# Two convolution blocks issued one step earlier, their writes put ahead of the reads, and one transposing 128x128 transfer beside the first loads

## Chip, cores, metric

One core of a Trainium2 chip. The metric is the device time of the program in microseconds (us), lower is better. Each timed run also leaves the span of the profiled part, which is about 1.8 us shorter than the time. A ratio below is the mean time of one kernel's fast runs over the mean of the other's fast runs of the same rounds, so not quite the ratio of the medians that are quoted beside it.

## The reference

```python
# attention part: a causal 7-tap convolution over the sequence, one softmaxed filter per head
x: (8, 4096, 192); weight: (8, 7)           # 8 heads of 24 channels
w = softmax(weight, axis=-1)
att[b, s, h] = sum_k w[h, k] * x_pad[b, s + k, h]     # zero padding of 6 in front
# MoE part, over the 32768 tokens
h = att @ w_in                              # 192 -> 2048
g = where(h > 0, h, exp(min(h, 0)) - 1)     # ELU
out = g @ w_out                             # 2048 -> 192
```

## The kernel before

The tokens are worked off in 32 super-tiles of 1024. Each has 16 steps; a step multiplies one block of 128 hidden columns into PSUM (`H<-att,w_in`), ScalarE takes the exponential, GpSimd clamps it, VectorE makes the ELU (`gT`), and the second product (`ops<-w_out,gT`) is interleaved. Between steps stand convolution blocks for later super-tiles, each for one half (`g`) of 512 tokens. Their results go to DRAM (`bounce`, in the profile `conv_slots`) and come back in another layout as `att`. Super-tile 0 has a path of its own at the start: x is loaded, cast, transposed and convolved on the spot.

```python
EARLY_CONV = {4: (1, 0), 7: (1, 1), 10: (2, 0)}   # after step n: convolve (super-tile, half)
...
def load_first(eng, k):                       # one half of the first x tile, DRAM to xf
    eng.dma_start(xf[:, k, :, :]..., x_flat[GS * k : GS * (k + 1), :]...).then_inc(s_xl[k], 16)

def read_att(eng, W, s, g):                   # three loads of 64 KB: att of half g
    m = 2 * s + g - 2
    W(s_dw[m % 4], 16 * (m // 4 + 1))         # the write of this half has landed
    for j in range(3):
        eng.dma_start(att[HP * g : HP * (g + 1), s % 2, j, :], src).then_inc(s_att[s % 2], 16)
...
def _sync(sy):
    sy.dma_start(wh[:], weight[:, :]).then_inc(s_wd, 16)
    load_first(sy, 1)                         # the other half is loaded by the ACT queue
    W(s_wp, 1)
    sy.dma_start(taps[:, :], zt[:, :]).then_inc(s_band, 16)
    W(s_band, 16)
    sy.dma_start(Tr[:, :, :], <tap matrix out of taps>).then_inc(s_band, 16)
    W(s_w[3], 16)
    sy.dma_start(w_in[HP:P, :, c0:c1], w_in[0:HP, :, c0:c1]).then_inc(s_wc, 16)
    for item in order:
        if item[0] == "c":                    # a convolution block m
            conv_read(W, m)                   # evacuated into csb
            sy.dma_start(bounce[...], csb[:, m % 4, :, :]).then_inc(s_dw[m % 4], 16)
            if m == 0 or g == 1:
                read_att(sy, W, s, g)         # waits for the write just issued to land
        ...
# TensorE, at the start
warm(9)                                       # matmuls on zeros
...                                           # broadcast of the taps into H
W(s_xha, 1); W(s_xh, 1)                       # both x halves cast
...                                           # transposes of x, then the first convolution
```

## Time and profile before

| | before |
|---|---|
| time, median of 2 runs | 750.02 us (749.67 to 750.38) |
| the profiled run | 752.16 us, span 750.4 us |
| TensorE busy | 737.4 us, 98% |
| longest wait on the path | 2.8 us, step 16 for `att` |

The prediction shows the chain and the waits. Added here, from the order of time of the same profile (start us, length us, engine, line, operation, tiles, count; in brackets the idle time before and what ended it), is the start-up of TensorE: the first convolution in two groups of matmuls, and step 0.

```profile
7.83 1.06 PE L648 MATMUL ops<-xT,Dg 64*128 64x256 bf16 x16 [0.34 <-ACT xT L438]
8.71 1.94 PE L648 MATMUL H<-xT,Dg 64*128 64x256 bf16 x32
11.21 0.82 PE L706 MATMUL H<-att,w_in 64*128 64x512 bf16 x6 [0.56 <-ACT att L447]
```

The first convolution runs from 7.83 to 10.65, 2.82 us, and step 0 starts at 11.21. Below, these two numbers are the measure of a start.

### The profile page before, as it was taken

What the parts mean: (1) busy time and instruction counts of PE and PEld (TensorE: products, weight loads), DVE (VectorE), ACT (ScalarE), POOL (GpSimd) and SP (SyncE); (2) the same over time, 40 slices, a digit from 0 to 9 for tenths busy, and PEclk for the clock granted to TensorE, in tenths of its full rate; (3) what the DMA queues carried; (4) which work ended last, traced back from release to release, by engine and by line L of the source; (5) the groups of instructions that cost most, each with busy time, mean ns of one, the idle gap of its engine ahead of it and who ended that gap; (6) DMA issues with size and microseconds to landing.
All of it is one profiled execution on the core that took longest, in us unless ns stands there. A gap on an engine that the chain in (4) does not pass through costs nothing.

```text
span 750.4 us, 32212 instructions
## 1 busy us (share of the span) xinstructions
PE 737.4 (98%) x13850; PEld 518.0 (69%) x13850; DVE 637.9 (85%) x1041; ACT 646.7 (86%) x1165; POOL 659.7 (88%) x1107
## 2 busy tenths in 40 slices
PE   7799999999999999999999999999999999999998
PEld 4377777777777777776776776777776777777666
DVE  5779888889888888898898898898898898888894
ACT  5788888888888888888989888888888888888884
POOL 8779889899899899899898898898898898998883
PEclk9999999999999999999999999999999999999999
DMA  9644434534435435435435435435345444345212
GB/s 171 126 86 99 99 92 103 107 84 104 90 97 107 106 75 115 86 90 113 102 81 117 84 92 110 93 93 115 77 101 107 88 102 103 87 103 105 60 44 65
DMA packets 107038, 72.79 MB, mean 97 GB/s; under 512 B 44552, under 2 KB 106640, under 8 KB 106896
## 3 DMA queue, kind: packets, MB, share of 16 engines
q1 hardware_dynamic: 66384, 54.47, 24.0%
q0 software_dynamic: 40224, 15.78, 19.6%
q8 instruction: 108, 1.77, 1.0%
q10 hardware_dynamic: 288, 0.49, 0.2%
q14 instruction: 34, 0.28, 0.1%
HBM read 44.78 MB, written 41.42 MB: 115 GB/s over the span
## 4 chain that ended last, share of the span: by engine, by line
PE 96%; DMA 2%; ACT 1%; DVE 0%; SPq 0%; issue 0%; POOL 0%
PE ops L741 45%; PE H L706 45%; PE H L679 5%; DMA conv_slots<-csb 1%; PE H L741 1%; DMA xf<-in_x_dram 1%; DMA att<-conv_slots 0%; SPq L334 0%; DVE gT L561 0%; ACT E L499 0%; PE H L648 0%; PE ops L648 0%; ACT csb L479 0%; POOL E L410 0%; ACT xT L438 0%
## 5 line engine op out<-in xcount | busy, mean ns | idle before, releaser
L561 DVE SCALAR_TENSOR_TENSOR gT<-E,H 128x512 f16<-128x512 f32 x1024 | 632.8, 681 | 96.7 <-POOL E L410 90.5
L410 POOL TENSOR_SCALAR E<-E 128x512 f32<-128x512 f32 x1024 | 602.7, 612 | 78.2 <-ACT E L499 72.6
L499 ACT ACTIVATE E<-H 128x512 f32<-128x512 f32 x1024 | 546.2, 606 | 87.8 <-PE H L706 79.2
L741 PEld LDWEIGHTS ops<-w_out,gT 64*128 64x128 f16 x8064 | 346.1, 94 | 107.0 <-ACT osb L470 10.9
L741 PE MATMUL ops<-w_out,gT 64*128 64x192 f16 x8064 | 417.9, 243 | 0.3
L706 PE MATMUL H<-att,w_in 64*128 64x512 bf16 x3072 | 408.7, 377 | 5.3 <-DMA att<-conv_slots 2.8
L706 PEld LDWEIGHTS H<-att,w_in 64*128 64x128 bf16 x3072 | 133.9, 94 | 102.9 <-issue 5.2
L479 ACT ACTIVATE csb<-H 128x1024 bf16<-128x1024 f32 x59 | 60.4, 1023 | 0.0
L470 ACT ACTIVATE osb<-ops 128x768 f32<-128x768 f32 x63 | 51.6, 819 | 6.2 <-PE ops L741 6.2
L362 POOL DMA_DIRECT2D xg<-in_x_dram x62 | 52.5, 847 | 0.4 <-issue 0.4
L679 PE MATMUL H<-Tr,xg 128*24 128x122 bf16 (+1 forms) x2360 | 38.6, 209 | 0.0
L679 PEld LDWEIGHTS H<-Tr,xg 128*24 128x24 bf16 x2360 | 29.6, 92 | 9.3 <-issue 9.3
L741 PE MATMUL H<-w_out,gT 64*128 64x192 f16 x128 | 5.9, 243 | 0.0
L572 DVE COPY osb<-H 128x192 f32<-128x192 f32 x1 | 0.4, 358 | 6.3 <-PE H L741 6.3
L741 PEld LDWEIGHTS H<-w_out,gT 64*128 64x128 f16 x128 | 5.3, 94 | 0.0
L592 PE MATMUL ops<-zw 128*128 128x512 bf16 x9 | 4.0, 631 | 1.2 <-DVE zw L511 1.2
L367 POOL DMA_DIRECT2D w_in<-in_moe_w_in_dram x7 | 4.6, 657 | 0.3 <-DMA wh<-in_weight_dram 0.3
L597 PE MATMUL ops<-zw 64*128 64x512 bf16 x12 | 2.3, 379 | 1.6 <-ACT csb L479 1.6
L479 ACT ACTIVATE csb<-ops 128x512 bf16<-128x512 f32 x6 | 3.8, 625 | 0.0
L592 PEld LDWEIGHTS ops<-zw 128*128 128x128 bf16 x9 | 1.2, 142 | 3.2 <-issue 1.9
L597 PEld LDWEIGHTS ops<-zw 64*128 64x128 bf16 x12 | 0.6, 93 | 3.0 <-ACT csb L479 2.6
L679 PEld LDWEIGHTS ops<-Tr,xg 128*24 128x24 bf16 x120 | 1.5, 92 | 1.3 <-issue 1.3
(47 smaller groups left out, 25.9 us busy)
## 6 DMA issues: line engine op xcount, KB each, us to landing
out_dram<-osb SPq DMA_DIRECT2D x126, 192.0 KB, 2.7
conv_slots<-csb SPq DMA_DIRECT2D x62, 256.0 KB, 2.5
att<-conv_slots SPq DMA_DIRECT2D x186, 64.0 KB
xg<-in_x_dram POOLq DMA_DIRECT2D x31, 240.0 KB, 5.1
xg<-in_x_dram POOLq DMA_DIRECT2D x31, 192.0 KB, 4.5
w_out<-in_moe_w_out_dram POOLq DMA_DIRECT2D x1, 768.0 KB, 14.3
w_in<-in_moe_w_in_dram POOLq DMA_DIRECT2D x2, 240.0 KB, 7.9
xf<-in_x_dram ACTq DMA_DIRECT2D x1, 384.0 KB, 3.2
```

The source lines that it names most:

```text
L362: g.dma_start(xg[:, b, w0:w1, :], src).then_inc(s_x[b][part - 1], 16)
L367: g.dma_start(w_in[HP * r : HP * (r + 1), :, c0:c1], moe_w_in.rearrange("(p j) f -> p j f", j=3)[:, :, c0:c1],).then_inc(s_w[k], 16)
L410: g.tensor_scalar(out=E[:, n % NE, u, :], in0=E[:, n % NE, u, :], scalar1=1.0, scalar2=0.0, op0=ALU.min, op1=ALU.max,).then_inc(s_clp)
L470: a.activation(osb[:, b, :, :, :].rearrange("p g k d -> p g (k d)"), ops[:, :, 0 : 2 * D], ACT.Copy,).then_inc(s_oev)
L479: return a.activation(csb[:, m % 4, b0:b1, :], conv_bank(m)[:, b0:b1, :], ACT.Copy)
L499: a.activation(E[:, n % NE, u, :], H[:, k, GS * u : GS * (u + 1)], ACT.Exp).then_inc(s_exp)
L561: v.scalar_tensor_tensor(out=gT[:, s % NG3, q, u, :], in0=E[:, n % NE, u, :], scalar=1.0, in1=H[:, slot_of_pair[n] % 3, GS * u : GS * (u + ...
L592: pe.matmul(ops[:, 0, :], zw[:, 0:P], zw[:], start=True, stop=True)
L597: pe.matmul(ops[:, r, :], zw[HP * r : HP * (r + 1), 0:P], zw[HP * r : HP * (r + 1), :], start=True, stop=True, tile_position=(HP * r, 0),)
L679: ins = pe.matmul(to[SLOT * q : SLOT * q + CPH, hb, o : o + nc_], xg[:, s % NXB, w, CPH * h : CPH * (h + 1)], Tr[:, h, CW - c0 - nc_ : CW ...
L706: ins = pe.matmul(H[:, k % 3, GS * r : GS * (r + 1)], w_in[HP * r : HP * (r + 1), j, FC * q : FC * (q + 1)], att[HP * r : HP * (r + 1), s ...
L741: ins = pe.matmul(acc[:, g, d0 : d0 + D], gT[HP * rt : HP * (rt + 1), t % NG3, q, g, t0 : t0 + P], w_out[HP * rt : HP * (rt + 1), q, :], s ...
```

## The change

Its intent: the write of half 1 shall no longer queue behind the reads of half 0, and both halves shall be ready earlier. A transposing transfer from SBUF to SBUF is added besides; nothing reads its result. Its source is a tile of zeros.

```diff
-EARLY_CONV = {4: (1, 0), 7: (1, 1), 10: (2, 0)}
+EARLY_CONV = {3: (1, 0), 6: (1, 1), 10: (2, 0)}
...
+        tt = sbuf("tt", [P, P], BF16)
...
+        s_tx = sema("s_tx")
...
             sy.dma_start(wh[:], weight[:, :]).then_inc(s_wd, 16)
+            W(s_zw, 1)
+            sy.dma_start_transpose(out=tt[:, 0:P], in_=zw[:, 0:P]).then_inc(s_tx, 16)
             load_first(sy, 1)
...
-                    if m == 0 or g == 1:
-
+                    if m == 1:
+                        read_att(sy, W, s, 0)
+                    if g == 1:
                         read_att(sy, W, s, g)
...
+            W(s_tx, 16)
```

## The prediction

> **What bounds the kernel now.** I read the page's engine table first, then the chain of work that ended last (whole, then its first 70 us), then the longest waits and the table by stretches of the same time, then the order of time around the stall, and last the DMA queues microsecond by microsecond.
>
> The engine table of the page:
>
> ```profile
> PE 737.4 (98%) x13850; PEld 518.0 (69%) x13850; DVE 637.9 (85%) x1041; ACT 646.7 (86%) x1165; POOL 659.7 (88%) x1107
> ```
>
> TensorE is busy for 737.4 of 750.4 us. From 43 us on the stretches show it busy without a gap, so nothing there can be shortened by moving transfers: the steady state is a block of fixed length, and the change can only move the moment at which it begins. All that matters lies before 43 us. The chain there (start, length, what):
>
> ```profile
> 1.26 4.12 DMA xf<-in_x_dram
> 5.37 0.02 issue
> 5.40 0.57 DVE xh L536
> ...
> 19.87 5.74 DMA conv_slots<-csb
> 25.61 0.02 issue
> 25.62 0.67 SPq L334
> ...
> 27.58 2.55 DMA conv_slots<-csb
> ...
> 31.40 3.55 DMA att<-conv_slots
> 34.95 0.05 issue
> 35.00 0.82 PE H L706 x6
> 35.82 0.78 PE ops L741 x12
> 36.60 1.28 PE H L706 x6
> 37.88 1.57 PE ops L741 x20
> 39.45 0.65 PE H L706 x6
> ```
>
> It begins with the second half of the first x load, on the sync queue, and later runs through that queue: write of conv half 0 (landed 25.61), three reads of half 0 (issued 25.62 to 27.54), only then the write of half 1, its three reads, and at 34.95 the data that step 16, the first of the second super-tile, needs. The longest waits and the stretches (length; busy us and count of PE, PEld, DVE, ACT, POOL; granted clock; DMA share; GB/s) show what it costs:
>
> ```profile
> PE H L706 <- DMA att<-conv_slots: 2.8, 1, 2.8
> ```
>
> ```profile
> 32.00:35.00 3.00, 0.15 (x5) 0.01 (x2) 2.35 (x4) 0.78 (x2) 1.52 (x3) 1.00 0.45 138
> 36.00:37.00 1.00, 1.00 (x12) 0.68 (x10) 0.00 (x0) 0.95 (x2) 0.46 (x1) 0.50 0.00 0
> ```
>
> TensorE stands from 32.15 to 35.00, 2.85 us. Afterwards its granted clock is 0.50, and the groups of the chain take twice as long: 0.78, 1.28 and 1.57 us, where the same groups later take 0.49, 0.65 and 0.82. That is another 1.67 us. The stall so costs 4.5 us in all.
>
> Was the order on the sync queue to blame? In the order of time:
>
> ```profile
> 23.38 0.65 ACT L479 ACTIVATE csb<-ops 128x512 bf16<-128x512 f32 x1
> 27.58 0.45 SPq L773 DMA_DIRECT2D conv_slots<-csb  x1
> ```
>
> Half 1 was evacuated at 24.03, but its write was issued at 27.58: 3.55 us behind a wait for the landing of half 0 and three reads. And why did half 0 need 5.74 us, where later writes take 2.5? The queues (packets, MB, share), first from 20 to 21 us, then from 22 to 23:
>
> ```profile
> q0 software_dynamic: 502, 0.19, 159.8%
> ```
>
> ```profile
> q1 hardware_dynamic: 155, 0.23, 73.6%
> ```
>
> Up to about 21 us the weight and x loads issued by GpSimd fill the engines, and the sync queue (q1) moves nothing, though its copy of w_in was issued at 17.82. The write of half 0 can't land much before 25 however early it is issued.
>
> **What the skill says.** (1) The Trainium skill, "VectorE: DVE Perf Modes", section "The three transpose paths", gives the crossbar DMA 1309 ns for 128x128 bf16. This trace has no transpose; its plain sync issues take 0.36 to 0.40 us. (2) "DMA: Bandwidth & Descriptors", section "Queues, rings and completion order": on each DMA engine descriptors are consumed in ring order. So a transfer put ahead of the x load on the same queue is served ahead of it. The trace agrees: the conv_taps write, issued at 3.61, landed at 5.75, after the x load before it at 5.38. (3) The same page, section "Rules for kernel authors", says a transpose next to ordinary DMAs needs nothing; so I expect no corruption and no pause of the other queues, which no run has shown yet. (4) "TensorE: Matmul & The Clock Gate", Part 1: the array falls to half its clock after an idle window of about 3.4 us. The trace agrees on the half clock, but 2.85 us of standing sufficed here, and the half clock lasted from about 35.9 to 39.2.
>
> **The change part by part.** *Convs one step earlier.* Half 0 moves from after step 4 to after step 3, half 1 from after step 7 to after step 6. The input is there: the GpSimd queue landed x for half 0 near 12.7 us (issue 5.11 plus 7.6) and for half 1 near 16.4 (7.61 plus 8.8). ScalarE is close to fully busy from 18 to 31 and does the same evacuations in another order, so half 0 is ready perhaps 0.65 us earlier, near 19.2, and half 1 near 23.4. The number of warming matmuls stays 12. By itself this buys almost nothing, because of the DMA backlog above. Value: about 0.
>
> *Writes ahead of reads.* Half 1 is now written as soon as evacuated: issue near 23.4 to 24, in the ring right behind half 0. At the 0.2 MB per us that q1 reaches there, 0.25 MB more land by about 27, not 30.13. Reads of half 0: from 25.6, three issues, 1.92 us, to 27.5. Reads of half 1: 1.9 to 2.2 us more, to about 29.5; the last lands 2.6 us after the end of its issue, as before (34.95 minus 32.33), so at about 32.1 instead of 34.95. TensorE's own arrival was 32.15. The stall of 2.85 us goes, and with it the half clock: minus 2.85 minus 1.67, or minus 4.5 us. The elementwise engines don't take its place: VectorE finishes step 15 at 34.35 in the trace before, when step 18 would first need that buffer at about 35.
>
> *The transpose.* It is issued on the sync queue between the first two loads. Its source is filled at 1.19 us and the queue is free at 1.20, so its wait is free. It holds the queue for between 0.45 us (a little over a plain issue) and 1.3 us (the skill's figure taken as issue time), and its 32 KB are ahead of the x load in the ring. That load is the head of the chain. Pushed back by 0.5 to 1.3 us, more of it meets the GpSimd loads, which begin at about 4 us; in that microsecond q1 fell from 0.28 to 0.11 MB. I estimate that the x load lands 1.2 us later (0.6 to 2.5). The chain from there to step 0 has no slack, since VectorE waited 1.8 us for it; so the whole start moves by that. The reads of half 1 stay near 32.1, being held by the DMA backlog, while TensorE arrives at step 16 near 33.3, so the delay also secures that no stall is left. The final wait for the transpose is over long before the end and costs nothing.
>
> Sum: 750.0 - 4.5 + 1.2 = 746.7; with 0.1 for a remnant of a stall, 746.8 us.
>
> **Rivals.** *The transpose is dear.* A queue entry of another kind may hold the sync queue or the engines for several us. Nothing in the trace before speaks for or against it. With 3 us the time is about 748.5, with 4.5 about 750; if it went as 2-byte pieces (16,384 elements, some 1,000 per engine), at the roughly 30 per us and engine that 244-byte packets reach at 8 to 9 us, it would be over 30 us and the kernel over 2% slower. The skill's 1309 ns speaks against that. *The wait moves instead of going.* If reads of half 1 queue behind its write or their issue slows, att lands at 33 to 34; since TensorE comes late by the transpose's delay, at most about 1 us of stall is left: 747 to 748. *A cold start.* TensorE stands from 5.27 to 6.10 now; with the x load late it stands 2 us or more, and a window there could halve the clock for some us: plus 1.5, about 748. *All hidden.* If the x load does not feel the transpose (q1 moved nothing before 3 us anyway, behind the other half on the ACT queue), the whole 4.5 us remain: 745.5.
>
> **Range and chances.** The gain of 4.5 is measured and bounded; the transpose is the uncertain term. Delays of 0 to about 4 us give 745.4 to 749.4, which I take as the 8-in-10 range. Two per cent is 15 us: a gain that big isn't there to be had, so faster has 0.01; slower needs the 2-byte case or a stalled queue, 0.05; within 2% is 0.94.
>
> **What would show it.** Right: the wait of L706's line for att is gone or under 1 us; the granted clock is 1.00 from 32 to 40; two conv_slots writes stand together ahead of six att issues on the sync queue; the first cast of xf on VectorE begins near 6.6 instead of 5.40, and step 0 near 12.4 instead of 11.21. Wrong: a transpose issue of several us; the xf cast later than 8 us; a remaining att wait over 2 us, with the clock at 0.50 after it; or gaps in the steady state, which would mean that the transpose does something lasting to the queues.

## More of the kernel before

The experiments were timed in rounds with runs of the kernel before: e1 to e4, then e5, e6, e7 and e9, and then e8 with e10 to e12, on another chip.

## The result, and the profile after

The changed kernel took 750.75 us (750.67 and 750.83) against 750.02 before; the ratio is 1.0011 with an interval of 0.9987 to 1.0035. That is the same time, within 2% as forecast, but outside the predicted range of 745.4 to 749.4.

The sync queue of the changed kernel, in order of time:

```profile
1.26 1.21 SPq L759 DMA_TRANSPOSE tt<-zw  x1
2.52 0.57 SPq L301 DMA_DIRECT2D xf<-in_x_dram  x1
...
21.84 4.54 SPq L777 DMA_DIRECT2D conv_slots<-csb  x2
26.91 3.83 SPq L336 DMA_DIRECT2D att<-conv_slots  x6
```

The order is as intended: two writes (the length of a merged row spans the pause between them), then six reads, the last issued by 30.74. The `att` wait is gone. In the same table of stretches that showed a clock of 0.50 before, the changed kernel has:

```profile
36.00:37.00 1.00, 1.00 (x20) 0.64 (x18) 0.91 (x3) 1.00 (x2) 1.00 (x3) 1.00 0.28 88
```

So the whole 4.5 us that the prediction read out of the profile before are gone. What came in their place is at the start. From the order of time of the changed kernel:

```profile
6.60 0.56 DVE L538 CAST xh<-xf 128x768 bf16<-128x768 f32 x1 [3.02 <-DMA xf<-in_x_dram]
...
9.03 1.83 PE L650 MATMUL ops<-xT,Dg 64*128 64x256 bf16 x16 [0.33 <-ACT xT L440]
10.62 2.88 PE L650 MATMUL H<-xT,Dg 64*128 64x256 bf16 x32
...
14.06 0.82 PE L708 MATMUL H<-att,w_in 64*128 64x512 bf16 x6 [0.56 <-ACT att L449]
```

The transpose holds the sync queue for 1.21 us and the x load is issued 1.26 us later. The cast of x starts at 6.60 instead of 5.40, 1.20 us late. The first convolution then takes 4.47 us instead of 2.82, and its first group 1.83 instead of 1.06. Step 0 starts at 14.06 instead of 11.21, 2.85 us late. The stretches of the changed kernel (the column before the last two is the granted clock) name the cause of the second part:

```profile
9.00:10.00 1.00, 0.97 (x11) 0.87 (x13) 0.20 (x1) 0.37 (x1) 1.00 (x2) 0.56 1.10 108
10.00:11.00 1.00, 1.00 (x13) 0.87 (x10) 0.00 (x0) 0.10 (x1) 1.00 (x2) 0.50 1.50 189
```

The sum of this pair of profiles closes: minus 2.85 (stall) minus 1.67 (half clock after it) plus 2.85 (late start) plus 0.1 (a slightly longer way from step 0 to step 16) is minus 1.57, and the spans differ by 1.5 us. But the timed runs do not show minus 1.5. The profiled run of before took 752.16 us, about 2 us more than its timed runs. Which of the two stands for the kernel had to be found out.

### The profile page after: what moved, and what is told of

Same layout as the page of the kernel before. It is cut to its first block, busy times and chain, and to the rows that moved or that the text cites. A ratio compares the mean times of both kernels' runs of the same rounds, so it can differ in the third digit from the quotient of the medians.

```text
span 748.9 us, 32213 instructions
## 1 busy us (share of the span) xinstructions
PE 737.1 (98%) x13850; PEld 518.0 (69%) x13850; DVE 637.8 (85%) x1041; ACT 646.9 (86%) x1165; POOL 659.3 (88%) x1107
## 4 chain that ended last, share of the span: by engine, by line
PE 96%; DMA 2%; ACT 1%; DVE 1%; issue 0%; POOL 0%; ACTq 0%
PE ops L743 45%; PE H L708 45%; PE H L681 5%; DMA Tr<-conv_taps 2%; PE H L743 1%; DVE gT L563 0%; DMA conv_taps<-zt 0%; ACT E L501 0%; ACT csb L481 0%; ACT L425 0%; PE ops L681 0%; POOL E L412 0%; PE ops L599 0%; ACTq L301 0%; DVE osb L574 0%
```

## Experiments

**The theory.** Step 16 starts at the later of two moments: when TensorE arrives (step 0 plus some 20.8 us), and when `att` of super-tile 1 lands. In the old order the landing is held near 35 us by the backlog of the first loads and by the queue order, whenever step 0 starts. The packed traces have the landing itself, as the last semaphore update of the six reads: 34.60 to 35.61 us in the five profiles of the old order, 31.06 to 33.12 in the nine of the new one. The new order takes it off the path; the transpose, standing ahead of the x load, delays step 0 by as much. *Rivals:* the order is worth nothing in usual runs (B); the transpose's delay simply adds, whatever the order (C); the half clock hangs on the window's phase alone and not on TensorE standing (D); a transpose costs wherever it is issued (E).

Eleven kernels left fourteen profiles: one each, but three of the kernel before and two of the changed one. The table is read from the order of time of TensorE and VectorE in each: start of the cast of the second x half, length of the first convolution, start of step 0 and of step 16, and from step 20 to the end of the span.

| profile | order | extra transfer | cast | first conv | step 0 | step 16 | 16 minus 0 | step 20 to end |
|---|---|---|---|---|---|---|---|---|
| before | old | none | 5.40 | 2.82 | 11.21 | 35.00 | 23.79 | 707.30 |
| e11_before_look | old | none | 4.98 | 4.09 | 12.38 | 34.85 | 22.47 | 707.41 |
| e12_before_look2 | old | none | 5.17 | 3.70 | 12.18 | 35.65 | 23.47 | 707.41 |
| e8_steps_only | old | none | 5.43 | 4.92 | 14.06 | 34.80 | 20.74 | 707.47 |
| e2_transpose_only | old | transpose ahead | 7.66 | 4.55 | 15.76 | 36.61 | 20.85 | 707.46 |
| e7_order_only | new | none | 5.34 | 3.93 | 12.59 | 33.44 | 20.85 | 707.33 |
| e1_no_transpose | new | none | 5.13 | 3.70 | 12.15 | 32.88 | 20.73 | 707.40 |
| e9_order_bridge | new | none | 5.45 | 2.82 | 11.89 | 33.22 | 21.33 | 707.36 |
| e10_idle_transpose | new | transpose, idle place | 4.97 | 2.82 | 10.78 | 33.39 | 22.61 | 707.37 |
| e6_late_transpose | new | transpose behind x load | 5.33 | 3.46 | 12.11 | 33.59 | 21.48 | 707.29 |
| e5_after_bridge | new | transpose ahead | 7.43 | 2.82 | 13.24 | 34.52 | 21.28 | 707.35 |
| after | new | transpose ahead | 6.60 | 4.47 | 14.06 | 35.10 | 21.04 | 707.38 |
| e4_after_again | new | transpose ahead | 7.08 | 4.40 | 14.80 | 35.63 | 20.83 | 707.44 |
| e3_plain_copy | new | plain copy ahead | 6.46 | 4.96 | 14.76 | 35.49 | 20.73 | 707.48 |

The last column is the same within 0.2 us in all fourteen: nothing after step 20 is touched by any of this, as predicted. Every difference is made before.

### e1_no_transpose: the change without the transpose

```diff
-            W(s_zw, 1)
-            sy.dma_start_transpose(out=tt[:, 0:P], in_=zw[:, 0:P]).then_inc(s_tx, 16)
             load_first(sy, 1)
```

> The change without the transpose (convs a step earlier and writes ahead of reads kept). Theory A (the order removes the 2.85 us stall; the transpose gave that back through a late x load and a half clock): no att wait, clock 1.00 from 32 to 40 us, step 0 at 11.2, time 750.0 - 2.85 + 0.1 = 747.2, and 745.6 if the runs of before have the half clock after the stall as its profile had. Rival B (in unprofiled runs the stall is hidden, the order is worth nothing): 749.5 to 750.5.

Measured: 748.61 us (748.02 to 749.1, 6 runs) against 750.23 of before in the same rounds (749.33 to 752.61, 11 runs); ratio 0.9972, interval 0.9956 to 0.9989. No `att` wait. So the order is worth something (B falls), but the mean fell by 2.2 us (750.75 to 748.57), not by 4.5 nor quite by the 2.85 of the stall, and the expected 747.2 was missed. (The waits of the three profiles of before, 2.85, 1.6 and 2.6 us, have a mean of 2.3.) The first convolution took 3.70 us here, so step 0 started at 12.15, not at 11.2: a slow start without any transpose.

### e4_after_again: the change, unaltered

No edit.

> The change again, unaltered, for an interval and for how the clock falls from run to run. Expected 750.2 to 750.9; xf cast at 6.6 us, half clock from about 9 to 12.7 us if the fall is regular, at another time or absent if it hangs on a free-running window.

Measured: 751.24 us (750.15 to 751.45, 6 runs), ratio to before 1.0005, interval 0.9988 to 1.0021. Its mean is 751.01, so against e1 the transpose costs 2.4 us. The cast started at 7.08; the first convolution took 4.40 us, though the clock column shows 1.00 all along in this run. It is the lengths of the matmuls that tell the half clock; the column can miss it. It shows 1.00 for any stretch before a trace's first clock record, and here that record comes at 13.15.

The lengths also tell that this half clock is not that of the first profile of the changed kernel. The 22 transposes of x just before the first convolution, here and there:

```profile
8.43 1.47 PE L630 MATMUL H<-ident,xh 128*64 128x128 bf16 x22
7.82 0.88 PE L630 MATMUL H<-ident,xh 128*64 128x128 bf16 x22
```

There the clock was full (0.88 us, as in the profile before) and fell at 9.13, after TensorE had stood for 1.92 us. Here the transposes were slow already (1.47): the clock had not fallen, it had not risen yet. Every trace begins at half clock, with the warming matmuls 0.43 us apart, where e2, e5 and e10 end theirs 0.22 us apart. The first record of full clock lies at 4.0 to 7.1 us in six profiles (before, after, e2, e5, e9, e10) and at 9.5 to 13.7 us, within the first convolution, in the other eight. It moves from run to run of one kernel: 5.17, 10.40 and 9.78 in the three profiles of before. Only in the changed kernel's first profile and in e2 (at 7.44, within a stand of 3.79 us) did a full clock fall again before or in the first convolution. In e11 TensorE stood for only 0.30 us there, and the clock rose late all the same; so for the eight late rises rival D fits better than the standing.

### e2_transpose_only: before plus the transpose

```diff
             sy.dma_start(wh[:], weight[:, :]).then_inc(s_wd, 16)
+            W(s_zw, 1)
+            sy.dma_start_transpose(out=tt[:, 0:P], in_=zw[:, 0:P]).then_inc(s_tx, 16)
             load_first(sy, 1)
```

> The kernel before with the transpose alone. Theory A: the start is late by 1.2 us, or by 2.85 with a half clock at 9 to 13 us, but the landing of att is held by the backlog of the loads and does not move, so the delay is eaten by the stall: stall 0.3 to 1.6 us instead of 2.85, time 750 to 750.8. Rival C (the delay simply adds): 751.2 to 752.9 with the stall still at 2.85.

Measured: 752.06 us (750.63 to 752.55, 6 runs), ratio 1.0014, interval 0.9995 to 1.0033. This is above the 750 to 750.8 of the theory and inside the range of C, so the number alone is a miss. The profile decides: its longest wait on a transfer is at the start,

```profile
DVE xh L538 <- DMA xf<-in_x_dram: 4.1, 1, 4.1
```

and there is no wait for `att` at all. Step 0 starts at 15.76, 3.4 to 4.6 us later than in the three profiles of before, yet step 16 only 1.0 to 1.8 us later (36.61 against 34.85 to 35.65). The stall ate the rest, as the theory says; the delay was only larger than expected, so more of it came out on the far side. C, which had the stall remain at 2.85, falls. The means agree: the transpose costs 1.0 us in the old order (751.78 against 750.75) and 2.4 us in the new one.

### e3_plain_copy: a plain copy in place of the transpose

```diff
-            sy.dma_start_transpose(out=tt[:, 0:P], in_=zw[:, 0:P]).then_inc(s_tx, 16)
+            sy.dma_start(out=tt[:, 0:P], in_=zw[:, 0:P]).then_inc(s_tx, 16)
```

> The change with a plain copy of the same 128x128 tile in place of the transpose. If the kind of transfer costs (issue of 1.21 us against some 0.4), the x load lands only about 0.4 to 0.6 us late, TensorE stands about 1.4 us before the transposes of x, the clock stays at 1.00, and the time is about 747.7. If any extra transfer there does it: 750 to 750.8, as the change.

Measured: 750.34 us (749.58 to 751.1, 6 runs), ratio 0.9996, interval 0.9979 to 1.0013. The sync queue of this profile:

```profile
1.26 0.57 SPq L759 DMA_DIRECT2D tt<-zw  x1
1.88 0.58 SPq L301 DMA_DIRECT2D xf<-in_x_dram  x1
```

The issue is half as long as the transpose's, and the x load goes out 0.64 us earlier, but the cast still starts at 6.46, 1.1 to 1.5 us later than in the three profiles of before. By means, the copy costs 1.8 us (750.37 against 748.57 of e1) where the transpose costs 2.4. So most of the price is that of any 32 KB transfer in front of the x load, and only some 0.6 us that of the kind; with spreads of 1.3 to 1.5 us and six runs each, that last figure is rough. My expectation of 747.7 missed for that reason.

### e5_after_bridge: the change with TensorE kept busy

```diff
+            warm(5)
             W(s_xha, 1)
             W(s_xh, 1)
```

> The change with five more warming matmuls between the tap broadcast and the x transposes, so that TensorE does not stand while it waits for the late x load. Theory A (part of the transpose's price is the half clock in the first convolution, 4.4 to 4.5 us where 2.8 is full speed): that stage falls to about 2.8 to 3.2 us, step 0 starts some 1.4 us earlier against the x cast, time about 749.5 to 749.9. Rival D (the half clock there hangs on the window's phase alone, not on TensorE standing): stage still 4.4 to 5 in most runs, time 751 as the change.

Measured: 750.96 us (750.03 to 752.12, 5 runs), ratio 1.0005, interval 0.9991 to 1.002. The profile of this kernel with a bridge, as the added matmuls are called below, shows the first convolution at full speed, 2.82 us, its first group again 1.06:

```profile
9.86 1.06 PE L651 MATMUL ops<-xT,Dg 64*128 64x256 bf16 x16 [0.33 <-ACT xT L440]
```

and the profiled run was the quickest of the five, 750.03. But the median did not move, and the expected 749.5 to 749.9 was missed. So the first convolution was fast in the run that was seen, in which the full clock came at 5.73, and on the whole nothing was gained; whether the bridge keeps a risen clock from falling, and whether D holds for the other four runs, can't be told, because only one run leaves a trace.

### e6_late_transpose: the transpose behind the x load

```diff
-            W(s_zw, 1)
-            sy.dma_start_transpose(...)
             load_first(sy, 1)
+            W(s_zw, 1)
+            sy.dma_start_transpose(...)
```

> The change with the transpose issued after the x load instead of ahead of it. Theory A (the price is the place on the queue, ahead of the x load): x cast near 5.2 to 5.6 us, the transpose hidden, time as without it, 748.3 to 748.9. Rival E (a transpose costs wherever it stands, by disturbing the other transfers): 750 or more, with the x cast late all the same.

Measured: 749.52 us (748.23 to 749.97, 5 runs), ratio 0.9985, interval 0.9971 to 0.9998. The cast starts at 5.33, on time. Against 751.01 for the transpose ahead of the load, its mean of 749.31 is 1.7 us lower, so the place on the queue is most of the price. It remains 0.9 us above the kernel without a transpose of the same rounds (e7, mean 748.42), more than the theory gave it. In this place the load of the tap matrix was issued at 6.46, as in the changed kernel, against 5.74 in e7, and the weight load of a convolution block waited 0.4 us for it; that explains a part at most, and was not tested by itself.

### e7_order_only: writes ahead of reads, nothing else

```diff
-                    if m == 0 or g == 1:
+                    if m == 1:
+                        read_att(sy, W, s, 0)
+                    if g == 1:
                         read_att(sy, W, s, g)
```

> The kernel before with the writes ahead of the reads alone; convs after steps 4 and 7 as before, no transpose. Theory A (the order is the whole gain, the earlier step nothing): no att wait, ramp from step 0 to step 16 about 20.9 us, time 748.2 to 749.0, as with both. If the earlier step carries a part: att wait of 0.5 to 1.3 us and 749.2 to 750.

Measured: 748.57 us (747.83 to 748.89, 5 runs), ratio 0.9973, interval 0.996 to 0.9986; as with both (0.9972). No `att` wait, 20.85 us from step 0 to step 16. The order is the whole gain, as far as intervals of about 1 us to either side can tell.

### e8_steps_only: convs a step earlier, nothing else

```diff
-EARLY_CONV = {4: (1, 0), 7: (1, 1), 10: (2, 0)}
+EARLY_CONV = {3: (1, 0), 6: (1, 1), 10: (2, 0)}
```

> The kernel before with the convs after steps 3 and 6 alone; the reads of half 0 still ahead of the write of half 1. Theory A (the earlier step is worth nothing, as the write of half 0 lands only when the backlog of loads has drained, near 25 us): time 749.9 to 750.8 as before, att wait still there, 1 to 3 us. If the step counts: 749.2 or less.

Measured: 750.15 us (749.4 to 752.6, 6 runs) against 750.71 (11 runs), ratio 0.9988, interval 0.9971 to 1.0006. No effect can be seen. The expected `att` wait was missing in the profile, because in this run the first convolution took 4.92 us and step 0 came at 14.06; TensorE arrived at 34.80, when `att` was just there (its last semaphore update is at 34.60). The write of half 1 was still issued only at 28.17. It is one more point for the landing near 35 us, and one more slow start without a transpose.

### e9_order_bridge: the new order, no transpose, TensorE kept busy

```diff
+            warm(3)
             W(s_xha, 1)
             W(s_xh, 1)
```

> No transpose, convs a step earlier, writes ahead of reads, and three warming matmuls more before the x transposes. Without them that kernel's first convolution took 3.70 us. Theory A: about 2.8 us, time 747.3 to 748.0, the best so far. Rival D: no difference from 748.6, or a little worse where the three matmuls at half clock hold up the transposes of x by up to 0.5 us.

Measured: 748.42 us (747.46 to 749.45, 5 runs), ratio 0.9972, interval 0.9956 to 0.9988. The first convolution took 2.82 us and step 0 came at 11.89, but step 16 at 33.22, no earlier than in e1 and e7: the way from step 0 to 16 grew to 21.33, with a 0.7 us wait for the tap matrix in it. The expected 747.3 to 748.0 was missed. In this profile a faster start was eaten by a wait for another of the first loads. It is level with e1 and e7, and no better.

### e10_idle_transpose: the transpose where the sync queue idles

```diff
             sy.dma_start(Tr[:, :, :], ...).then_inc(s_band, 16)
+            W(s_zw, 1)
+            sy.dma_start_transpose(out=tt[:, 0:P], in_=zw[:, 0:P]).then_inc(s_tx, 16)
             c0, c1 = WCOLS[3]
             W(s_w[3], 16)
```

(and taken away from ahead of the x load)

> The change with the transpose moved to where the sync queue waits for nothing but the weights, behind the load of the tap matrix, at about 6 us. Theory A: wholly hidden, x cast near 5.3 us, time 748.3 to 748.9, as without a transpose and under both kernels. Rival E (it costs wherever it stands): 749.3 or more, as when it was issued right behind the x load (749.3 on average).

Measured: 749.1 us (748.21 to 749.87, 6 runs) against 750.71, ratio 0.997, interval 0.9957 to 0.9984. Its queue row and a wait:

```profile
6.01 1.33 SPq L767 DMA_TRANSPOSE tt<-zw  x1
```

```profile
PE H L708 <- DMA w_in<-w_in: 1.0, 1, 1.0
```

The transpose still takes 1.33 us of the queue, but the queue has nothing else to do until 19 us. The kernel does all that the changed one does, and its ratio to before is that of the kernels without a transpose (0.9972 and 0.9973). They were run at other times. So E, by which a transpose costs the same wherever it is issued, falls. The median itself, 749.1, lies between the two expected ranges, so a cost of some tenths is not excluded. In this profile the start was the quickest of all (step 0 at 10.78), and yet step 16 came at 33.39: a step now waited 1.0 us for the copy of `w_in`, the next thing that the load backlog holds. Whether the transpose itself made that copy late (issued at 19.09, against 17.6 to 18.7 in the profiles without an extra transfer) was not tested.

### e11_before_look and e12_before_look2: before, looked at twice more

No edit.

> The kernel before, unaltered, for one more profile. The first one came from a run of 752.16 us, while most runs take 749.3 to 750.5. If the att landing is held by the backlog of loads, a usual run has a slow first convolution (3.5 to 4.5 us instead of 2.82), so a later step 0, a shorter att wait (1 to 2 us) and no half clock after it; span 747.6 to 748.8. In a run of 752 the same picture as in the first profile.

> The same kernel once more, for the same reason: across the profiles of before, step 16 should start within some 0.5 us of 35.0 whether step 0 came at 11.2 or later, and the half clock should be there only with an att wait near 2.8 us.

Measured: 750.48 and 751.27 us (one run each). From the chain of the first, the start of step 0 and of step 16, and its wait:

```profile
12.38 0.84 PE H L706 x6
...
34.85 0.82 PE H L706 x6
35.67 0.49 PE ops L741 x12
```

```profile
PE H L706 <- DMA att<-conv_slots: 1.6, 1, 1.6
```

and of the second:

```profile
12.18 0.84 PE H L706 x6
...
35.65 0.82 PE H L706 x6
36.48 0.49 PE ops L741 x12
```

```profile
PE H L706 <- DMA att<-conv_slots: 2.6, 1, 2.6
```

In both, the first convolution was slow (4.09 and 3.70 us), step 0 about 1 us later than in the first profile, the wait 1.6 and 2.6 us, and there is no half clock after it: the twelve matmuls behind step 16 take 0.49 us, not the 0.78 of the first profile. Step 16 starts at 34.85 to 35.65 in all three, whatever step 0 did (35.65 is a little outside the expected half microsecond around 35.0). The first profile was of a run of the less frequent kind: quick start, longest wait, half clock after it, 752.16 us. Seven of the 31 timed runs of before took 752 us or more; that they looked the same is not shown. The 31 runs of before range from 748.97 to 753.25, and those of e1, e7 and e9 only from 747.46 to 749.45.

## Why the prediction was wrong, point by point

- **What bounds the kernel.** Right. From step 20 to the end all fourteen profiles agree within 0.2 us, and the whole matter is settled before 43 us.
- **Where the `att` landing comes from.** Right. The queue order holds half 1: the order alone removes the wait (e7), the earlier step does nothing that can be seen (e8). The landing predicted near 32.1 came at 32.50 in the changed kernel. That the backlog of loads holds half 0 is argued, since no run took the loads away; the traces show that its write, issued at 19.87 to 24.43 us, landed at 25.61 to 26.73 in all five profiles of the old order.
- **The size of the gain: wrong.** The sum put "750.0 - 4.5 + 1.2". The 4.5 were read in a run of 752.16 us and taken off a median of 750.02 that other runs had given. "The gain of 4.5 is measured and bounded" was true of that one run only. The two further looks at before have 1.6 and 2.6 us of wait and no half clock after it. Measured over 5 and 6 runs, the order gives 2.2 to 2.3 us of mean time (e1: 750.75 to 748.57; e7: 750.68 to 748.42). This term alone is about 2.2 us of the miss. What failed is the step from the wait to its worth: the wait of one run, with a half clock that only that run showed, was taken for that of all.
- **The transpose: the way right, the size half of it.** Issue time 1.21 us (predicted 0.45 to 1.3) and cast 1.20 us late (predicted 1.2) in the first profile, but 7.08, 7.43 and 7.66 in three others; the mean of the four is 2.0 us later than that of the nine profiles with nothing ahead of the load (4.97 to 5.45). The whole price is 2.4 us (e4 against e1), not 1.2. About 1.8 of it is paid by a plain copy in the same place too (e3).
- **The rival "a cold start" came true in the changed kernel's first profile and in e2,** where the clock fell after or within a longer stand, and had been left out of the sum. With a transfer ahead of the x load and no bridge, the first convolution took 4.40 to 4.96 us in four profiles; in the other two of these, e3 and e4, the clock had not risen yet. Without such a transfer it also ran slow in most, 2.82 to 4.92 over eight profiles that had no bridge, each time by a late rise. So only a part of that slowness belongs to the transpose, and how large a part is not shown. The prediction took the quick start of the one profile for the usual one.
- **"The final wait costs nothing", "nothing lasting to the queues".** Right; the last column of the table shows it.
- **Two readings were slightly off,** without effect on the sum: the plain sync issues of the first 20 us take 0.30 to 0.73 us, not 0.36 to 0.40, and TensorE stood from 5.37, not 5.27, since one small matmul ran in between.

With the two terms as measured the same sum reads 750.7 (mean of before, first call) minus 2.2 plus 2.4, or 750.9, where the change was measured at 751.0 in that call. This is no second check, since both terms are differences of the means of that call. What stays open is what sets the moment at which the clock first rises, which in most profiles decided how fast the first convolution ran, and the 0.9 us by which the transpose behind the x load is slower than none.

## What to carry to other kernels

A stall behind a fixed landing absorbs any delay ahead of it: taking the stall away and adding a delay upstream cancel, so ask of each extra transfer what it stands in front of, and issue it where its queue idles anyway. A gain read from one profile may be taken only off the time of that same run; if the profiled run lies 2 us from the timed ones, look at a second profile before subtracting. On one queue, issue every write that is ready before a read that has to wait.

## What the Trainium skill lacked or had wrong

- "VectorE: DVE Perf Modes", section "The three transpose paths", gives 1309 ns for the crossbar transpose and does not say whether that is issue or landing. Here the issue held the sync queue for 1.20 to 1.33 us and the data landed 3.0 to 3.3 us after the issue when it stood ahead of the x load, and 9.1 us after it among the full load queues (e10); a plain copy of the same tile held it 0.57 us and landed after 3.2 us. Queue time, not landing, is where the two differ.
- "TensorE: Matmul & The Clock Gate", Part 1, speaks of some 3.4 us of activity for full speed and of idleness for half speed, on a free-running window. In agreement with that, the half clock lasted 3.41 us in the profile before and 3.41 in the changed kernel's, and the first full clock came at 4.0 to 13.7 us after the same start. But a stand of 1.92 us was followed by a fall (the changed kernel) and so was one of 2.85 us (before), while one of 2.6 us was not (e12). After the nine warming matmuls, 4.0 us of unbroken work in most profiles, the first convolution was still slow in ten of the twelve profiles without a bridge (3.46 to 4.96 us against 2.82): a warm-up of that length does not secure full speed. The page warns that the recorded clock events can't be trusted; in these fourteen traces they agree with the lengths of the first matmuls to about 0.1 us. What misled was the clock column, which read 1.00 before the first record, in a run whose first convolution took 4.40 us.
- "DMA: Bandwidth & Descriptors", section "Queues, rings and completion order", has the engines go round between queues packet by packet. In the profile before, the sync queue's copy of `w_in`, issued at 17.82, had not begun before 21 us (the queue moved one packet from 17 to 22), while the GpSimd queue moved 0.19 MB in each microsecond. That section does not say that a queue can stand so long beside a full one; the cause was not tested.
- "DMA: Bandwidth & Descriptors", section "Rules for kernel authors", says that a transpose next to ordinary DMAs needs nothing. All outputs were correct, which agrees as far as the other transfers go. The transposed tile was of zeros and was read by nothing, so no run shows that its own result was right.
